# Clustered attention feeding a gated FFN: one pool of eight PSUM banks, five seven-product sets in each later group, and an order read from a table

## The chip, the cores and the metric

The kernel runs on one core of one Trainium2 chip. The metric is device time in microseconds of one execution. TensorE (PE in the profile; its weight loads are PEld), VectorE (DVE), ScalarE (ACT), GpSimd (POOL) and SyncE (SP) each run their own queue of instructions in order and wait for each other through semaphores. TensorE writes its products into PSUM, which has eight banks of 512 float32 per partition; VectorE and ScalarE read them there.

## The reference

There are 4 batches, 8 heads, 768 positions and a head size of 64; 16 centroids per head; d_model 512 and d_ff 1536; 3072 tokens.

```python
q_assign = argmax(einsum(q / |q|, c / |c|));  k_assign = argmax(einsum(k / |k|, c / |c|))
scores = q @ k.T / 8, and -1e9 where q_assign != k_assign
attn   = softmax(scores) @ v                      # [B, H, S, D]
x      = attn.transpose(0, 2, 1, 3).reshape(B * S, H * D)
out    = (sigmoid(x @ w_gate) * (x @ w_val)) @ w_out
```

## The kernel before

**Attention.** The work of a batch `b` is cut into two *groups* of queries (`gr` 0 and 1: even and odd chunks of 128 queries), and each group into four head pairs `p`. One group of one pair is a *block*: 3 chunks of queries, 384 columns (in batch 0 some blocks are split into 2 and 1 chunks, so that there are 36 blocks in all). `prepare`, `prepare_pair` and `prepare_first` turn the queries and keys, find each position's cluster and append it as extra rows of the operands; the products of `scored` in `prepare` (line 687) are the cluster scores for two pairs of heads. `attend` works through the 12 units (head, key chunk) of a block, two units at a time: score products (line 1008) into a tile `sc` of two PSUM banks, one exponential on ScalarE over both banks (line 1032, 768 elements), value products with the exponentials as weights (line 1059, 65 columns each) into the bank `av`. At the end of a block VectorE takes the reciprocal of the row sums out of `av` (line 1084), scales (line 1089), and the result is turned into `x`, by DMA in most blocks.

**FFN.** When the four pairs of a group are done, `feed` multiplies `x` with the gate and value weights. The common form takes one 128-row chunk `fc` of d_ff at a time: four gate products and four value products (line 1396, 384 columns each), Tanh on ScalarE (line 1561) and one VectorE instruction that gates (line 1572). The other form, `seven_products`, takes two chunks `fa`, `fa + 1` at once as a 2 x 2 by 2 x 2 block product with seven products in place of eight: seven times four matmuls of 192 columns (line 1474), three copies of banks on ScalarE (line 1493) and three additions on VectorE (line 1505), then two Tanh (line 1512) and two gating instructions (line 1520). One such *set* replaces sixteen matmuls of 384 columns, two Tanh and two gating instructions. It needs differences of `x` (line 1436, four per group) and sums of the weights, which `sum_up_weights` makes once (line 1377). Before, the groups have 0, 0, 2, 2, 2, 3, 3 and 2 sets, 14 in all; the temporary tiles `pu` and `p5` of a set exist twice each. `project` then multiplies with `w_out`, two 128-token chunks at a time, itself with seven products (line 1271), sums of `hT` on VectorE (line 1241), halvings on ScalarE (line 1289) and sums on VectorE (line 1296), and stores.

**PSUM and order.** The eight banks are two `sc` tiles of two banks, one `av` bank and three `ring` banks for everything else. All steps are tasks of the class `Order`. It runs a list schedule on planned durations: on each engine the task that can start first goes first, and among those within 0.02 us of it the one with the smallest `due`. DMA landing times are computed by `transfers`, and eight rounds of both are made before the instructions are written out:

```python
for _ in range(8):
    order = self.schedule()
    self.transfers()
order = self.schedule()
```

The queue of every engine is therefore fixed when the program is built. A task that acquires a buffer waits for the last user of the buffer's slot; `ring` takes the slot that comes free first, the other tags go round in turn.

Of the kernel before, what the change touches and what calls it, by code (L numbers as in the profile page):

```python
# [9 lines left out]
FP = mybir.dt.float32  # L10
# [3 lines left out]
AX = mybir.AxisListType  # L14

# [23 lines left out]
class Order:  # L39
# [54 lines left out]
    def transfers(self):  # L94


        begin = self.DMA_START
        todo = sorted((t for t in self.tasks if t.dma), key=lambda t: t.start + begin[t.eng])
        queues, left, now, n = {}, {}, 0.0, 0
        while n < len(todo) or any(queues.values()):  # L100
            heads = [ts[0] for ts in queues.values() if ts]
            come = todo[n].start + begin[todo[n].eng] if n < len(todo) else float("inf")
            if heads:
                total = sum(t.pkt for t in heads)
                step = min(min(left[t] * total / t.pkt for t in heads), max(0.0, come - now))
                for t in heads:
                    left[t] -= step * t.pkt / total
                    if left[t] < 1e-6:
                        t.landing = now + step + self.DMA_LAND - t.start
                        queues[t.eng].remove(t)  # L110
                now += step
            else:
                now = max(now, come)
            while n < len(todo) and todo[n].start + begin[todo[n].eng] <= now + 1e-9:
                queues.setdefault(todo[n].eng, []).append(todo[n])
                left[todo[n]] = todo[n].dma
                n += 1
# [92 lines left out]
def kernel(  # L210
# [45 lines left out]
        "xn": ([128, QCH, 128], HP), "x": ([128, NDC, 512], HP), "hT": ([128, NFC, 512], HP),  # L256
        "gt": ([128, 512], FP), "p5": ([128, 384], FP), "out2": ([128, 2, DM], FP),
        "sc": ([128, 2, 512], FP), "av": ([128, 512], FP), "ring": ([128, 512], FP),
    }
    PSUM = bass.MemoryType.PSUM  # L260
    SPACES = {"sc": PSUM, "av": PSUM, "ring": PSUM}
# [4 lines left out]
            (banks if tag in SPACES else const).tile(*SHAPES[tag], name=f"{tag}{i}")  # L266
            for i in range(n)
        ]
        for tag, n in BUFS.items()
# [7 lines left out]
    def take(buf):  # L277
        buf.tile = kept[buf.tag][buf.slot]
        return buf.tile

# [12 lines left out]
    WP = (2, 4, 8)  # L293
    wss = const.tile([128, len(WP), 4, 2, 2, 128], HP, name="wss")
# [56 lines left out]
    w_ring = Buf("av")  # L351
# [66 lines left out]
    c_ring = Buf("av")  # L418
# [160 lines left out]
    def prepare(b, grp, due, step, act=(), queues=("SP",), split=False):  # L579
# [101 lines left out]
        rg = Buf("sc")  # L681

        def scored():
            ps = take(rg)
            for half in range(2):
                for g, (p, nm) in enumerate(sides):
                    nc.tensor.matmul(  # L687
                        out=ps[32 * g : 32 * g + 32, half, :QB], lhsT=cblk[:, 2 * p + half, :],
                        rhs=t32[p, nm].tile[:, half * QB : (half + 1) * QB], start=True, stop=True,
                    )  # L690
# [3 lines left out]
            due, lat=0.3, acq=[rg], uses=[t32[x] for x in sides],  # L694
        )
        for half in range(2):
# [10 lines left out]
            def back(cols=cols, oh=oh, half=half):  # L707
# [5 lines left out]
                lambda t1=t1, half=half: turn_scores(take(t1)[:n], rg.tile[:n, half, :QB]),  # L713
                [cl], due, lat=0.11, acq=[t1], uses=[rg],
# [268 lines left out]
    def attend(block, at, slot):  # L983
# [15 lines left out]
        for i, (e, j) in enumerate(some):  # L999
            kb = aug[b, p][j % 2]  # L1000

            def score(i=i, e=e, j=j, kb=kb):
                ps = sc.tile if i else take(sc)
                to = (
                    ps.rearrange("p u c -> p (u c)")[:, i * N : (i + 1) * N] if together % 2
                    else ps[:, i // per, i % per * N : (i % per + 1) * N]
                )
                nc.tensor.matmul(  # L1008
                    out=to,
                    lhsT=kb.tile[0:80, 0, e * QB + j // 2 * 128 : e * QB + (j // 2 + 1) * 128],  # L1010
                    rhs=qb_.tile[0:80, 1, e * QB + c0 * 128 : e * QB + c0 * 128 + N],
                    start=True, stop=True,
                )
# [6 lines left out]
                    acq=[] if i else [sc], uses=[kb, qb_] + ([sc] if i else []),  # L1020
# [5 lines left out]
        def exponentials():  # L1026
            to, of = take(es)[:, : together * N], sc.tile
            if together % 2:
                of = of.rearrange("p u c -> p (u c)")[:, : together * N]
            else:  # L1030
                to, of = to.rearrange("p (u c) -> p u c", u=2), of[:, :, : per * N]
# [12 lines left out]
            [*t1, c_small, c3], due, lat=0.16, acq=[es], uses=[sc],  # L1044
        )
        first, last = at == 0, at + together == len(UNITS)
        if first:
            avb[block] = Buf("av")
        av = avb[block]
# [3 lines left out]
        def value():  # L1053
# [16 lines left out]
            seq=exps[-1:], acq=[av] if first else [], uses=[es] + ([] if first else [av]),  # L1070
# [52 lines left out]
        t5 = od.add("DVE", 0.12 + 0.113 * nq, norm, [t4], due - 7.0, lat=0.14, acq=[xn], uses=[av, rr])  # L1123
# [62 lines left out]
    def project(b, one, two, final, many, end):  # L1186
# [11 lines left out]
        if many:  # L1198
# [11 lines left out]
            r1, r2 = Buf("sc"), Buf("sc")  # L1210
            X, Y, Z = (lambda: r1.tile[:, 0, :HM]), (lambda: r2.tile[:, 0, :HM]), (lambda: r1.tile[:, 1, :HM])
        else:
            s1, s2, s4, hf, df = (Buf(x) for x in ("s22", "s11", "s12", "half", "diff"))
            t_s1, t_s2, t_s4, t_hf, t_df = (lambda x=x: x.tile for x in (s1, s2, s4, hf, df))
            r1, r2 = Buf("ring"), Buf("ring")
            X, Y, Z = (lambda: r1.tile[:, :HM]), (lambda: r2.tile[:, :HM]), (lambda: r1.tile[:, HM:])

# [82 lines left out]
        def out_part(r, m):  # L1300
# [8 lines left out]
            Z, many, lambda: a(0, 1), lambda i: w_part(i, 1, 0), lambda i: done1[: 2 * i], [], [r1, *hs], runs=parts,  # L1309
# [11 lines left out]
        k2 = halved(lambda: t_df()[:, 1], X, [p6], [], [r1, df], due=due)  # L1321
# [42 lines left out]
    Q2 = {"DVE": nc.vector, "POOL": nc.gpsimd}  # L1364

    def sum_up_weights(n, fa, due):
        g1, g2, v1, v2 = weights(fa)
        s2, s3, s4, s1 = (wss[:, n, i] for i in range(4))
        before = [wload["g"][fa // FPG], wload["v"][fa // FPG]]
        tasks = []  # L1370
        for to, x, y, op in (
            (s1, v1, v2, ALU.add), (s3, g1, v1, ALU.subtract), (s2, s1, g1, ALU.subtract), (s4, g2, s2, ALU.subtract),
        ):
            tasks.append(
                od.add(
                    "DVE", 0.4 if "DVE" == "DVE" else 1.65,
                    lambda to=to, x=x, y=y, op=op: Q2["DVE"].tensor_tensor(to, x, y, op),
                    before + tasks[-1:], due, lat=0.12, both=True,
                )
            )  # L1380
        wsums_of[fa] = [tasks[-1]]

    def feed(b, gr, work):
# [27 lines left out]
        if not wsums_of:  # L1411
# [33 lines left out]
        def seven_products(fa, work):  # L1445
            n = WP.index(fa)
            g1, g2, v1, v2 = weights(fa)
            s2, s3, s4, s1 = (wss[:, n, i] for i in range(4))
            if (b, gr) == (B - 1, 1):
                X = Y = Buf("sc")  # L1450
            else:
                X, Y = Buf("ring"), Buf("ring")
            Z = Buf("ring")
# [3 lines left out]
            def bank(r_, y=0):  # L1457
                return (r_.tile[:, y] if r_.tag == "sc" else r_.tile)[:, :N]
# [7 lines left out]
            def product(r_, new, w_, x_, deps, step, y=0):  # L1466

                def go():
                    if new and not (y and X is Y):
                        take(r_)  # L1470
                    ps = by_chunk(bank(r_, y))
# [9 lines left out]
                    due_ffn(work + step * 0.8), lat=0.25, acq=[r_] if new and not (y and X is Y) else [],  # L1481
                    uses=[xb, tb] + ([r_] if not new or y and X is Y else []), seq=free + ([m1] if y and new else []),
                )

            def copied(i, r_, m, eng="ACT", y=0):
# [3 lines left out]
                def go():  # L1489
                    if new:  # L1490
                        take(to)
                    if eng == "ACT":
                        nc.scalar.copy(held(i), bank(r_, y))  # L1493
                    else:
                        nc.vector.tensor_copy(held(i), bank(r_, y))
# [6 lines left out]
            def added(i, r_, deps, y=0):  # L1502
                return od.add(
                    "DVE", 0.45,
                    lambda: nc.vector.tensor_tensor(held(i), bank(r_, y), held(i), ALU.add), deps,  # L1505
# [27 lines left out]
            m5 = product(Y, True, s1, lambda: t_part(0), [], 0.02, 1)  # L1533
            m2 = product(Z, True, g2, lambda: x_part(1, 0), [], 0.04)
            k1 = copied(0, X, m1)
            k5 = copied(2, Y, m5, "ACT", 1)
            a11 = added(0, Z, [m2, k1])
            m6 = product(X, False, s2, lambda: t_part(1), [k1], 1)
            m3 = product(Y, False, s4, lambda: x_part(1, 1), [k5], 1.02, 1)
            k2 = copied(1, X, m6)  # L1540
            a12 = added(1, Y, [m3, k2], 1)
# [7 lines left out]
        for fc in range(NFC):  # L1549
# [17 lines left out]
            rv, v1 = proj("v", fc, due, [g1])  # L1567

# [97 lines left out]
    z_ring = Buf("av")  # L1666
# [43 lines left out]
```

## Time and profile before

| | |
|---|---|
| time, median of 3 runs | 313.62 us (313.61 to 313.62) |
| the profiled execution's own time | 313.22 us |
| its span, first to last instruction | 311.4 us |
| TensorE clock granted | 1.00 throughout |
| PE busy | 303.7 us, 3251 matmuls |
| PEld busy | 222.8 us |
| ACT busy | 238.2 us, 389 instructions |
| DVE busy | 217.8 us, 532 instructions |
| POOL busy | 77.0 us |

The profiled execution's own time is 1.8 us longer than its span and 0.4 us shorter than the median of the timed runs. A busy time is the time in which at least one instruction of the engine was under way. Successive instructions of an engine overlap by their start-up and their tail, so the distance from one start to the next is shorter than the duration that a row shows; both are used below, the first as *pace*, the second as *duration*.

### The profile page before, as it was taken

The numbers are of one execution on the slowest core, as the hardware profiler recorded it, in microseconds if no ns is written. First come the engines' busy times: TensorE is split into PE (matmuls) and PEld (weight loads), VectorE is DVE, ScalarE is ACT, GpSimd is POOL, SyncE is SP. The second block draws the span as 40 slices with busy tenths as digits, with TensorE's granted clock in tenths as the row PEclk, the third lists the DMA queues.
The fourth block names the chain that finished last, engine by engine and source line by source line (L and its number), as shares of the span: only waits on it lengthen the run. The fifth ranks groups of instructions, "written<-read, shape, count | busy, mean of one in ns | idle before, by whom it ended". The sixth has DMA issues, their size and how long they took to land.

```text
span 311.4 us, 8300 instructions
## 1 busy us (share of the span) xinstructions
PE 303.7 (98%) x3251; PEld 222.8 (72%) x3251; DVE 217.8 (70%) x532; ACT 238.2 (76%) x389; POOL 77.0 (25%) x110
## 2 busy tenths in 40 slices
PE   8998999999999999999999999999999999999995
PEld 3676888544687867757776877757777888778784
DVE  4999945899865739885376938977375824685862
ACT  4799999334999989868997777959899778945531
POOL 4997756751012302440002200570000000000000
PEclk9999999999999999999999999999999999999999
DMA  6999999993356966891465673978300121001003
GB/s 217 359 272 212 214 175 129 163 154 72 69 99 142 114 100 204 106 114 45 107 105 84 101 182 99 103 101 73 96 4 14 48 83 46 15 2 67 2 1 135
DMA packets 97286, 34.49 MB, mean 111 GB/s; under 512 B 83120, under 2 KB 93024, under 8 KB 97248
## 3 DMA queue, kind: packets, MB, share of 16 engines
q1 hardware_dynamic: 72192, 24.57, 34.6%
q0 software_dynamic: 24336, 8.65, 26.4%
q10 hardware_dynamic: 720, 0.75, 0.7%
q8 instruction: 25, 0.41, 0.6%
q14 instruction: 13, 0.11, 0.2%
HBM read 28.34 MB, written 6.29 MB: 111 GB/s over the span
## 4 chain that ended last, share of the span: by engine, by line
PE 92%; ACT 4%; DVE 1%; DMA 1%; issue 0%; SPq 0%; ACTq 0%
PE ring L1396 29%; PE sc L1008 19%; PE ring L1271 16%; PE av L1059 11%; PE ring L1474 9%; ACT es L1032 3%; PE sc L687 3%; PE sc L1271 1%; PE sc L1474 1%; DMA nat<-in_k_dram 1%; PE ring L795 1%; PE ring L617 1%; PE ring L835 1%; PE ring L903 0%; PE ring L948 0%
## 5 line engine op out<-in xcount | busy, mean ns | idle before, releaser
L1032 ACT ACTIVATE es<-sc,nbias 128x768 f16<-128x768 f32 (+1 forms) x189 | 167.8, 925 | 21.2 <-PE sc L1008 20.4
L1059 PEld LDWEIGHTS <-es 128*128 128x128 f16 x1152 | 53.6, 97 | 13.6
L1059 PE MATMUL av<-vp,es 128*128 128x65 f16 x1152 | 58.6, 193 | 0.0
L1396 PE MATMUL ring<-x,wv 128*128 128x384 f16 (+2 forms) x272 | 55.4, 326 | 0.1
L1396 PE MATMUL ring<-x,wg 128*128 128x384 f16 (+2 forms) x272 | 55.3, 326 | 0.0
L1561 ACT ACTIVATE gt<-ring 128x384 f32<-128x384 f32 (+2 forms) x68 | 33.9, 499 | 28.0 <-PE ring L1396 24.8
L1572 DVE SCALAR_TENSOR_TENSOR hT<-gt,ring 128x384 f16<-128x384 f32 (+2 forms) x68 | 37.2, 548 | 24.3 <-PE ring L1396 20.7
L650 POOL CAST even<-t 128x768 f16<-128x768 f32 x24 | 20.6, 875 | 119.9 <-DVE t L595 47.1
L1396 PEld LDWEIGHTS <-wv 128*128 128x128 f16 x272 | 24.7, 97 | 16.5 <-issue 2.1
L1396 PEld LDWEIGHTS <-wg 128*128 128x128 f16 x272 | 24.4, 97 | 14.6 <-issue 0.8
L1271 PEld LDWEIGHTS <-hT 128*128 128x128 f16 x294 | 27.3, 97 | 5.0
L1008 PE MATMUL sc<-even 80*128 80x384 f16 (+2 forms) x120 | 26.1, 293 | 1.6 <-ACT es L1032 0.9
L1008 PE MATMUL sc<-odd 80*128 80x384 f16 x96 | 26.6, 325 | 0.1
L1271 PE MATMUL ring<-wo,hT 128*128 128x256 f16 x198 | 26.4, 272 | 0.0
L1008 PE MATMUL sc<-even,odd 80*128 80x384 f16 (+2 forms) x120 | 26.1, 293 | 0.0
L1008 PE MATMUL sc<-odd,even 80*128 80x384 f16 x96 | 25.8, 326 | 0.0
L1008 PEld LDWEIGHTS <-even 80*128 80x128 f16 x216 | 19.7, 98 | 8.2 <-issue 3.1
L1008 PEld LDWEIGHTS <-odd 80*128 80x128 f16 x216 | 19.7, 98 | 7.3 <-issue 2.1
L595 DVE STREAM_TRANSPOSE t<-nat 128x384 f32<-128x384 f32 x40 | 21.1, 553 | 1.2 <-DMA nat<-in_q_dram 0.9
L1505 DVE TENSOR_TENSOR nat<-ring,nat 128x384 f32<-128x384 f32 x26 | 13.9, 548 | 10.8 <-ACT nat L1493 9.2
L1296 DVE SCALAR_TENSOR_TENSOR out<-ring,diff 128x256 f32<-128x256 f32 x22 | 9.3, 422 | 17.0 <-PE ring L1271 16.8
L1271 PEld LDWEIGHTS <-s 128*128 128x128 f16 x198 | 18.7, 97 | 3.4
(133 smaller groups left out, 444.8 us busy)
## 6 DMA issues: line engine op xcount, KB each, us to landing
out_dram<-out SPq DMA_DIRECT2D x22, 256.0 KB, 2.2
nat<-in_k_dram SPq DMA_DIRECT2D x32, 96.0 KB, 3.0
nat<-in_q_dram SPq DMA_DIRECT2D x32, 96.0 KB, 3.0
odd<-even SPq DMA_DIRECT2D x12, 192.0 KB, 2.9
vp<-in_v_dram POOLq DMA_DIRECT2D x24, 96.0 KB, 4.6
nat<-in_k_dram SPq DMA_DIRECT2D x5, 384.0 KB, 7.7
nat<-in_q_dram SPq DMA_DIRECT2D x5, 384.0 KB, 6.2
nat<-in_v_dram SPq DMA_DIRECT2D x4, 384.0 KB, 7.9
```

The costliest lines, as they stand in the source:

```text
L595: nc.vector.transpose(t[:, half * QB : (half + 1) * QB].rearrange("p (c x) -> p c x", x=128), blocks_[:, half],)
L650: nc.gpsimd.tensor_copy(t[:, NM[nm], cols], t32[p, nm].tile[:, cols])
L687: nc.tensor.matmul(out=ps[32 * g : 32 * g + 32, half, :QB], lhsT=cblk[:, 2 * p + half, :], rhs=t32[p, nm].tile[:, half * QB : (half + 1) * ...
L1008: nc.tensor.matmul(out=to, lhsT=kb.tile[0:80, 0, e * QB + j // 2 * 128 : e * QB + (j // 2 + 1) * 128], rhs=qb_.tile[0:80, 1, e * QB + c0 * ...
L1032: i = nc.scalar.activation(to, of, AF.Exp, bias=nbias, scale=D ** -0.5 if quarters(b, p) else scale,).ins
L1059: nc.tensor.matmul(out=av.tile[:, g : g + D + 1], lhsT=es.tile[:, i * N + c * 128 : i * N + (c + 1) * 128], rhs=vp[:, e, j, :], start=firs ...
L1271: nc.tensor.matmul(out=ps[:, lo:hi], lhsT=left_()[:, i], rhs=right(i)[:, lo:hi], start=new and i == 0, stop=i == NFC // 2 - 1, skip_group_ ...
L1396: nc.tensor.matmul(out=ps[:, :N], lhsT=ws[fc // FPG][:, dcc, fc % FPG, :], rhs=xb.tile[:, dcc, :N], start=(dcc == 0), stop=(dcc == NDC - 1),)
L1474: nc.tensor.matmul(out=ps[:, f], lhsT=w_[:, d, f], rhs=x_()[:, d], start=new and not (f or d), stop=d == 1, skip_group_check=True,)
L1505: lambda: nc.vector.tensor_tensor(held(i), bank(r_, y), held(i), ALU.add), deps,
L1561: lambda rg=rg, gt=gt: nc.scalar.activation(take(gt)[:, :N], rg.tile[:, :N], AF.Tanh, scale=0.5),
L1572: nc.vector.scalar_tensor_tensor(t[:, fc, :N], gt.tile[:, :N], 1.0, rv.tile[:, :N], ALU.add, ALU.mult)
```

## The change

- **One pool.** All eight banks are one tensor `big`, and `ring` has eight slots. A step of two score units, and the cluster scores of `prepare`, acquire any two free slots; the two banks are read as `big[:, lo : hi + 1 : hi - lo]`, so that an exponential or a transposition steps from one bank to the other by whatever distance they have. `sc` (2) and `av` (1) remain as tokens without memory: still at most two score steps and one value bank are open at a time. Exponentials over one bank only are possible too; the first block takes 2, 4, 4 and 2 units at a time in place of 3, 3, 3 and 3.
- **Five sets.** `WP` grows from (2, 4, 8) to (2, 4, 6, 8, 10), and every group of batches 1 to 3 uses all five: 30 sets in place of 14. One of the four weight sums is now written over the value weights `v1`, after the last ordinary use of them in batch 0; the other three have a place of their own, 5 x 3 in place of 3 x 4. `hT` tile 0 is 384 columns wide in place of 512.
- **The order.** `transfers` and its rounds go. Each task gets its rank from a table `PLACES` as `due`, and each DMA its landing time from a table `LANDINGS`; one list schedule with these gives the queues.

The arithmetic of the result, the DMAs and their sizes stay as they are. The core of the diff:

```diff
+PLACES = """ 0 1 9 2 16 3 5 15 ... """        # one rank for each task
+LANDINGS = """ 2.6 3.45 4.13 ... """          # one landing time for each DMA
     def run(self):
-        for _ in range(8):
-            order = self.schedule()
-            self.transfers()
+        places, landings = ([float(x) for x in text.split()] for text in (PLACES, LANDINGS))
+        moved = [t for t in self.tasks if t.dma]
+        for t, at in zip(self.tasks, places):
+            t.due = at
+        for t, landing in zip(moved, landings):
+            t.landing = landing
         order = self.schedule()
...
-        "sc": 2, "av": 1, "ring": 3, "p5": 2,
+        "ring": 8, "p5": 2, "sc": 2, "av": 1,
...
+    big = banks.tile([128, BUFS["ring"], 512], FP, name="ring")
+    kept["ring"] = [big[:, i] for i in range(BUFS["ring"])]
...
+    def both_banks(two):
+        lo, hi = sorted(buf.slot for buf in two)
+        return big[:, lo : hi + 1 : hi - lo]
...
-    WP = (2, 4, 8)
-    wss = const.tile([128, len(WP), 4, 2, 2, 128], HP, name="wss")
+    WP = (2, 4, 6, 8, 10)
+    wss = const.tile([128, len(WP), 3, 2, 2, 128], HP, name="wss")
...
-            together = 3
-        per = together // 2
+            together = 4 if 0 < at < len(UNITS) - 2 else 2
+        per = together // 2 if together * N > 512 else together
...
-        sc, es = Buf("sc"), Buf("es")
+        turn_, sc, es = Buf("sc"), [Buf("ring") for _ in range(together // per)], Buf("es")
...
-            (s1, v1, v2, ALU.add), (s3, g1, v1, ALU.subtract), (s2, s1, g1, ALU.subtract), (s4, g2, s2, ALU.subtract),
+            (s1, v1, v2, ALU.add, []), (s2, s1, g1, ALU.subtract, []), (s4, g2, s2, ALU.subtract, []),
+            (v1, g1, v1, ALU.subtract, raw_users[fa] + raw_users[fa + 1]),
...
-        seven = WP[: {(0, 0): 0, (0, 1): 0, (1, 0): 2, (1, 1): 2, (2, 0): 2, (2, 1): 3, (3, 0): 3, (3, 1): 2}[b, gr]]
-        if (b, gr) == (B - 1, 1):
-            seven = (2, 4)
+        seven = WP if b else ()
...
-            if (b, gr) == (B - 1, 1):
-                X = Y = Buf("sc")
-            else:
-                X, Y = Buf("ring"), Buf("ring")
-            Z = Buf("ring")
+            s3 = v1
+            X, Y, Z = Buf("ring"), Buf("ring"), Buf("ring")
```

More of the change, by code (lines that the diff above doesn't have):

```diff
@@ L92, in free_slots @@
         return max(x[0] for x in ends), [x[1] for x in ends]
[L94 to L111, printed above, removed]
-            else:
[L113 to L117, printed above, removed]
-    def run(self):
-        for _ in range(8):
-            order = self.schedule()
-            self.transfers()
+    def run(self):
+        places, landings = ([float(x) for x in text.split()] for text in (PLACES, LANDINGS))
+        moved = [t for t in self.tasks if t.dma]
+        assert len(places) == len(self.tasks) and len(landings) == len(moved)
+        for t, at in zip(self.tasks, places):
+            t.due = at
+        for t, landing in zip(moved, landings):
+            t.landing = landing
         order = self.schedule()
@@ L1002, in score @@
             def score(i=i, e=e, j=j, kb=kb):
[L1003 to L1007, printed above, removed]
+                to = big[:, sorted(x.slot for x in sc)[i // per], i % per * N : (i % per + 1) * N]
                 nc.tensor.matmul(
@@ L1464, in by_chunk, with product @@
                 return t.rearrange("p (f t) -> p f t", f=2)
-            def product(r_, new, w_, x_, deps, step, y=0):
+            def product(r_, new, w_, x_, deps, step):
                 def go():
-                    if new and not (y and X is Y):
+                    if new:
                         take(r_)
-                    ps = by_chunk(bank(r_, y))
+                    ps = by_chunk(bank(r_))
                     for f in range(2):
@@ L1664 @@
             work = feed(b, gr, work)
-    z_ring = Buf("av")
+    z_ring = Buf("ring")
     def zeros_in_between():
```

100 lines of the change are left out of this document (50 added, 50 removed), and 104 rows, old and new, of tables (LANDINGS, PLACES).

## The prediction

> **What bounds the kernel now.** First the page: busy times, and the chain that ended last.
>
> ```profile
> PE 303.7 (98%) x3251; PEld 222.8 (72%) x3251; DVE 217.8 (70%) x532; ACT 238.2 (76%) x389; POOL 77.0 (25%) x110
> ...
> PE 92%; ACT 4%; DVE 1%; DMA 1%; issue 0%; SPq 0%; ACTq 0%
> ```
>
> TensorE is busy almost throughout and carries 92% of the chain; ScalarE's 4% is early. Since busy time is an average, I next asked for busy time by windows.
>
> ```profile
> 10.00:20.00 10.00, 9.38 (x119) 6.57 (x118) 9.52 (x25) 8.60 (x12) 9.77 (x15) 1.00 1.07 365
> 20.00:30.00 10.00, 9.43 (x130) 7.32 (x129) 9.24 (x26) 9.68 (x13) 8.88 (x13) 1.00 1.20 202
> 30.00:40.00 10.00, 9.49 (x145) 8.33 (x144) 8.73 (x26) 10.00 (x14) 6.88 (x9) 1.00 1.23 211
> 190.00:200.00 10.00, 10.00 (x125) 8.35 (x123) 9.93 (x25) 10.00 (x20) 3.33 (x4) 1.00 0.59 84
> 280.00:290.00 10.00, 9.50 (x92) 8.17 (x91) 6.13 (x14) 5.38 (x14) 0.00 (x0) 1.00 0.14 52
> ```
>
> The columns after the width are PE, PEld, DVE, ACT and POOL. Three stages differ. From 10 to 40 us PE lacks 0.62, 0.57 and 0.51 us, beside a full ScalarE. Later, as from 190 to 200, PE is full; ScalarE and VectorE can be full beside it. Near the end PE waits again, with nobody full. So less PE work pays from about 40 us on, if the others can follow. The next view is the chain in order of time, for PE's pace.
>
> ```profile
> 55.82 1.43 PE sc L687 x16
> ...
> 120.16 0.66 PE ring L1474 x8
> ...
> 159.53 1.30 PE ring L1396 x8
> ```
>
> Back to back, a 192-column matmul takes 0.66 / 8 = 0.0825 us and a 384-column one 1.30 / 8 = 0.1625. The paces of ScalarE and VectorE come from their timelines, start to start:
>
> ```profile
> 119.13 0.49 ACT L1561 ACTIVATE gt<-ring 128x384 f32<-128x384 f32 x1
> 119.50 1.70 ACT L1032 ACTIVATE es<-sc,nbias 128x768 f16<-128x768 f32 x2
> 121.07 0.51 ACT L1493 COPY nat<-ring 128x384 f32<-128x384 f32 x1
> 121.43 0.53 ACT L1493 COPY p<-ring 128x384 f32<-128x384 f32 x1
> 121.80 0.96 ACT L1032 ACTIVATE es<-sc,nbias 128x768 f16<-128x768 f32 x1
> 122.60 0.53 ACT L1493 COPY nat<-ring 128x384 f32<-128x384 f32 x1
> 122.95 0.60 ACT L1512 ACTIVATE nat<-nat 128x384 f32<-128x384 f32 x1
> 123.38 0.96 ACT L1032 ACTIVATE es<-sc,nbias 128x768 f16<-128x768 f32 x1
> ```
>
> ```profile
> 291.96 0.54 DVE L1572 SCALAR_TENSOR_TENSOR hT<-gt,ring 128x384 f16<-128x384 f32 x1
> 292.43 0.55 DVE L1520 SCALAR_TENSOR_TENSOR hT<-nat,p 128x384 f16<-128x384 f32 x1
> 292.89 0.54 DVE L1520 SCALAR_TENSOR_TENSOR hT<-nat,sc 128x384 f16<-128x384 f32 x1
> ```
>
> An exponential of 768 takes (121.07 - 119.50) / 2 = 0.785, a copy 0.365, a Tanh out of PSUM 0.37, one within SBUF 0.43; a VectorE instruction of 384 float32 takes 0.465.
>
> **The sets.** One set takes 28 x 0.0825 = 2.31 us of PE in place of 16 x 0.1625 = 2.60. Sixteen more sets: 16 x 0.29 = **-4.64 us**, all of it in stages where PE is full.
>
> They cost ScalarE 3 copies and 2 Tanh, 3 x 0.365 + 2 x 0.43 = 1.955 us, in place of 2 x 0.37 = 0.74: 16 x 1.215 = +19.4 us. They cost VectorE five instructions in place of two: 16 x 3 x 0.465 = +22.3 us, and eight more weight sums, under 0.47 each, +3.7. Neither is on the path while PE covers it, so I count a later group (four blocks and one feed). For value products I need one more pace; the fence also holds the waits near the end.
>
> ```profile
> 273.24 0.34 PE L1059 MATMUL av<-vp,es 128*128 128x65 f16 x6
> ...
> 274.40 0.53 PE L1059 MATMUL av<-vp,es 128*128 128x65 f16 x12
> ...
> 276.80 0.33 PE L1097 MATMUL ring<-ident,xn 128*128 128x128 f16 x3 [0.25 <-DVE hT L1520]
> ...
> 288.00 0.49 PE L1474 MATMUL sc<-nat,wss 128*128 128x192 f16 x4 [0.50 <-DVE nat L1505]
> ```
>
> Six more value products take 0.19 us, 0.032 each. PE: 48 score products x 0.1625 = 7.8, 144 value products x 0.032 = 4.6, five sets 11.55, two ordinary chunks 16 x 0.1625 = 2.6, the output with 1.5 x 42 matmuls at two thirds of 0.1625, 6.8: together 33.3 us. ScalarE: 24 x 0.785 = 18.8, sets 9.8, two gates 0.7, six halvings under 0.37 each, 2.2: 31.5 us, or 94%. With the present 2.33 sets on average it is 28.3 of 34.1, 83%. PE stays the bound, with a thin cover: 1.8 us a group.
>
> The cover is not even. In the order of instructions of the changed program, counted between the ends of blocks at these paces, ScalarE's work exceeds PE's in four later stretches, by 1.3, 0.6, 1.4 and 1.6 us, 4.9 in all. In the present order there is one such stretch (8.4 against 7.6, before the 31st block ends), and PE shows no wait in it: four `es` buffers let ScalarE run up to 4 x 0.785 = 3.1 us ahead. Bounds 0 and 4.9; nearest is that stretch without a wait, so I take **+0.3**.
>
> **The early stage.** The reciprocals at the ends of the sixth and twelfth block:
>
> ```profile
> 33.56 0.17 DVE L1084 RECIPROCAL rr<-av 128x4 f32<-128x4 f32 x1
> ...
> 54.58 0.19 DVE L1084 RECIPROCAL rr<-av 128x6 f32<-128x6 f32 x1
> ```
>
> These 21.0 us are ScalarE's: 24 exponentials x 0.785 = 18.8 and eight 256-wide gates make 21.0. PE's queue holds 19.8 us there. The changed order puts 22.0 us of PE work beside 21.3 of ScalarE's: the first cluster scores of batch 1 (the 1.43 us at 55.82) move to just behind the sixth block, and two blocks of batch 1 now stand ahead of the long ordinary feed, where PE had 29.1 us beside ScalarE's 11.2 (now 24.5 beside 10.4). PE work done beside exponentials need not be done later: I take **-1.0** of the 1.2 between 21.0 and 19.8. Bounds: 0, if data for the moved steps come late, and -2.2, if another 1.0 of the 1.7 us of waits between 10 and 40 us goes.
>
> The moved cluster scores also move their VectorE chain and, on SP, the shift and the eight row copies, which now queue ahead of batch 1's quarter loads; on POOL the loads for the second half of batch 1 come behind one cast more. Behind those wait the second cluster scores, which stand at the same place of PE's order as now (59 us of PE work in, 60 now), in the ordinary feed, which has other products for PE: 0, at most +1.
>
> **Start, pool, sums.** The first exponential waits for two score products of 256 columns in place of three, -0.1. Exponentials already step over two banks at 0.785; a longer stride I price at 0, both ways. With `sc` and `av` kept as tokens the pool lets no third score step in, so alone it gains nothing in attention; it serves the sets, whose three banks came out of three `ring` slots. The weight sums stand behind the last ordinary use of `v1`, in batch 0's feed: 0.
>
> **The end.** The last feed has no exponentials beside it. From the conversion of `x` that follows the products at 276.80 to the last gating, VectorE's queue holds 15.0 us now and PE's 20.3 to its last product; changed, 20.6 and 21.3. The slack falls from 5.3 to 0.7 us. With 5.3 PE waited 0.25 + 0.50; three sets more, with one such 0.50 each, would be 1.5, and double that is my upper bound. But PE now has output products of the group before between the sets, so I take **+0.6**, bounds 0 and +3.
>
> **Sum.** -4.64 + 0.3 - 1.0 - 0.1 + 0.6 = -4.84 us. The profiled execution took 313.22, 1.8 more than its span and 0.4 under the median of 313.62; the former gives 308.4, the latter, which I forecast, **308.8**.
>
> **Rivals.** The rows on which they rest, groups by shape:
>
> ```profile
> L1032 ACT ACTIVATE es<-sc,nbias 128x768 f16<-128x768 f32 x180 | 158.5, 915 | 20.9 <-PE sc L1008 20.1
> ...
> L1474 PEld LDWEIGHTS <-wss 128*128 128x128 f16 x224 | 19.1, 97 | 2.8 <-issue 0.6
> ...
> L1493 ACT COPY nat<-ring 128x384 f32<-128x384 f32 x24 | 12.2, 508 | 0.4 <-PE ring L1474 0.4
> ```
>
> *The four stretches are not absorbed* (0.13): up to 4.6 us more, 311 to 313.4, say 312.2. For it: order and buffers are fixed. Against it: the present stretch.
>
> *ScalarE becomes the bound; slower* (0.10). The place is the six later groups. An instruction that waits for a bank or for VectorE costs its duration and not its pace: 24 x 0.915 + 5 x (3 x 0.508 + 2 x 0.60) + 2 x 0.49 + 2.2 = 38.8 us a group against 31.5. It passes PE's 33.3 once a quarter of ScalarE's instructions wait so. At a half it is 35.15, and 6 x 1.85 = 11 us on the 308.5 that remain without the +0.3 give 319.6. For it: a set is a chain PE, ScalarE, PE, ScalarE, PE, VectorE, PE, VectorE, and `pu` and `p5` allow two at a time. Against it: from 190 to 200 us, with sets, ScalarE is full and PE too.
>
> *The weight loads set the pace of 192-column matmuls* (0.02). A load takes 0.097 us, more than 0.0825. If they did not overlap, a set would take 28 x 0.097 = 2.72 us, 0.12 more than 2.60: 16 x 0.12 = +1.9, with the other terms 315.3. The row at 120.16 is against it. The Trainium skill speaks for something like it: "TensorE: Matmul & The Clock Gate", Back-to-back issue gap, gives sustained streams of load and matmul about 81 ns each at 128 columns and 131 at 512; by a straight line between them, an estimate of mine, 192 columns would take 89 and 384 take 114, and sixteen sets would cost 10.7 us rather than save any. The trace, with 82.5 and 162.5, disagrees.
>
> *More goes early* (0.07): all 1.7 us of waits before 40 us and nothing lost at the end, 306.0.
>
> *The pool and the table bring nothing*: -4.64 and the two losses, 309.9, which lies in my own case (0.68).
>
> **Numbers.** My own case reaches from 306.7 (-2.2 early, no losses) to 311.2 (the end at +3). With half of the larger gain and most of the unabsorbed stretches the range is 306.2 to 312.6; left out are 0.12 slower, 0.03 and 0.04. A difference of 0.2%, 0.6 us, is about what a measurement can tell from none. Faster: 0.68 + 0.07 + 0.10 of the stretches = 0.85; same 0.03; slower 0.12.
>
> **What would show it.** Right: the new row of set products with 840 matmuls and about 0.33 us per four back to back; ScalarE about 19 us busier and VectorE 25; the sixth block's end near 33 us and the fourteenth's near 66 us, PE full from there to about 270 us; waits of PE on VectorE's additions at the end of 1 to 2 us. Wrong: waits of PE on exponentials or `L1512` after 100 us of more than 1 us in all (ScalarE as the bound), waits on cluster scores before 75 us (late data), or four set products taking more than 0.35 us back to back.

## The result, and the profile after

| kernel | median of its runs, us | lowest to highest | executions |
|---|---|---|---|
| before, beside the changed kernel | 313.62 | 313.37 to 313.62 | 4 |
| changed | 424.71 | 420.15 to 427.52 | 4 |

The changed kernel takes 1.343 times as long, 95% interval 1.3377 to 1.3483, where I had forecast 308.8 us. Two of the four executions, at 427.4 and 427.5 us, ran at a lower granted clock than the others; ratios, sums and the table of experiments leave such executions out, so that this kernel counts with 421.1 us below, and two others with 318.7 (319.7 in the statements) and 631.2. The profiled execution took 422.06 us, its span is 420.3. These are its busy times, the granted clock in 40 slices, and the chain that ended last:

```profile
PE 339.7 (81%) x3443; PEld 250.4 (60%) x3443; DVE 246.2 (59%) x588; ACT 265.7 (63%) x437; POOL 77.8 (18%) x110
...
PEclk9985565999999985899799998999989999999999
...
PE 52%; ACT 27%; DVE 11%; issue 4%; SPq 2%; DMA 2%; POOL 1%; ACTq 0%; DVEq 0%; POOLq 0%
ACT es L1123 23%; PE ring L1099 13%; PE ring L1558 11%; PE ring L1360 9%; PE ring L1485 8%; PE ring L1150 7%; PE ring L782 2%; SPq L429 2%; DVE nat L1589 2%; DVE hT L1604 1%; ACT nat L1596 1%; DVE hT L1657 1%; DMA x<-xn 1%; DVE xn L1180 1%; PE ring L712 1%
```

TensorE fell from 98% to 81% busy, and no other engine rose: ScalarE went from 76% to 63%. The busy times of ScalarE and VectorE grew by 27.5 and 28.4 us (I had 19.4 and 26.0). Part of that is instructions that stand apart and no longer overlap: in the kernel without the waits, below, the growth is 17.9 and 24.1. No engine has become the bound; they stand still in turn. ScalarE has 27% of the chain in place of 4%, nearly all of it in the exponentials. The waits, longest sums first (us in total, times, longest):

```profile
PE ring L1099 <- ACT es L1123: 29.6, 40, 1.4
...
ACT es L1123 <- PE ring L1099: 24.9, 34, 2.2
...
DVE hT L1657 <- ACT es L1123: 18.9, 8, 9.0
...
PE ring L1558 <- ACT es L1123: 15.0, 20, 1.1
...
ACT es L1123 <- PE ring L1485: 12.2, 12, 2.2
```

The third, fourth and fifth rows make no sense as data flow. A set's products (L1558) don't use the exponentials, an exponential doesn't use ordinary FFN products (L1485), and a gating instruction on VectorE (L1657) uses neither. All that the two sides share is that they touch PSUM. A bank that is handed on can make such a wait too, but of all the waits that the built program draws between these pairs of lines only 1 of 11 (third row), 5 of 26 (fourth) and 0 of 17 (fifth) join instructions with a bank in common. The exponentials themselves, in the groups by shape, are no slower than the 915 ns before:

```profile
L1123 ACT ACTIVATE es<-ring,nbias 128x768 f16<-128x768 f32 x176 | 155.4, 902 | 75.7 <-PE ring L1099 15.5 <-PE ring L1150 13.8 <-PE ring L1485 12.2
```

The windows of 10 us (after the width: PE, PEld, DVE, ACT, POOL, then the granted clock) show a second thing:

```profile
10.00:20.00 10.00, 8.97 (x105) 5.96 (x105) 9.13 (x23) 8.16 (x12) 9.22 (x13) 1.00 1.09 347
30.00:40.00 10.00, 7.11 (x62) 5.13 (x61) 3.94 (x11) 4.44 (x4) 0.30 (x1) 0.50 1.22 197
160.00:170.00 10.00, 7.35 (x42) 4.32 (x41) 2.42 (x5) 4.50 (x7) 0.83 (x1) 0.50 0.18 49
```

Where PE has long gaps its granted clock falls to 0.50, and then the products that do run take longer. In the last of these windows four 384-column products last from 166.69 to the next start at 167.97, 0.32 us each, against the 0.1625 of the kernel before:

```profile
166.69 1.48 PE L1485 MATMUL ring<-x,wg 128*128 128x384 f16 x4
167.97 0.52 PE L1099 MATMUL ring<-odd 80*128 80x384 f16 x1
```

### The profile page after: what moved, and what is told of

Same layout as the page of the kernel before. It is cut to its first block, busy times and chain, and to the rows that moved or that the text cites. A ratio compares the mean times of both kernels' runs of the same rounds, so it can differ in the third digit from the quotient of the medians.

```text
span 420.3 us, 8801 instructions
## 1 busy us (share of the span) xinstructions
PE 339.7 (81%) x3443; PEld 250.4 (60%) x3443; DVE 246.2 (59%) x588; ACT 265.7 (63%) x437; POOL 77.8 (18%) x110
## 4 chain that ended last, share of the span: by engine, by line
PE 52%; ACT 27%; DVE 11%; issue 4%; SPq 2%; DMA 2%; POOL 1%; ACTq 0%; DVEq 0%; POOLq 0%
ACT es L1123 23%; PE ring L1099 13%; PE ring L1558 11%; PE ring L1360 9%; PE ring L1485 8%; PE ring L1150 7%; PE ring L782 2%; SPq L429 2%; DVE nat L1589 2%; DVE hT L1604 1%; ACT nat L1596 1%; DVE hT L1657 1%; DMA x<-xn 1%; DVE xn L1180 1%; PE ring L712 1%
## 5 line engine op out<-in xcount | busy, mean ns | idle before, releaser
L1123 ACT ACTIVATE es<-ring,nbias 128x768 f16<-128x768 f32 (+2 forms) x189 | 168.8, 912 | 91.3 <-PE ring L1099 24.9
L1150 PE MATMUL ring<-vp,es 128*128 128x65 f16 x1152 | 63.0, 202 | 12.2 <-ACT es L1123 12.0
L1657 DVE SCALAR_TENSOR_TENSOR hT<-gt,ring 128x256 f16<-128x256 f32 (+2 forms) x36 | 19.5, 551 | 37.9 <-ACT es L1123 18.9
L1558 PEld LDWEIGHTS <-wss 128*128 128x128 f16 x360 | 31.0, 98 | 11.8 <-issue 9.8
L1099 PE MATMUL ring<-even 80*128 80x384 f16 (+2 forms) x120 | 29.8, 321 | 9.6 <-ACT es L1123 6.7
L1099 PE MATMUL ring<-even,odd 80*128 80x384 f16 (+2 forms) x120 | 30.4, 326 | 7.5 <-ACT es L1123 7.5
L1485 PE MATMUL ring<-x,wg 128*128 128x256 f16 (+2 forms) x144 | 32.3, 355 | 4.6 <-ACT es L1123 4.1
L1558 PE MATMUL ring<-x,wg 128*128 128x192 f16 x240 | 30.1, 251 | 6.6 <-ACT es L1123 5.3
L1558 PE MATMUL ring<-nat,wv 128*128 128x192 f16 x240 | 29.8, 247 | 6.7 <-ACT es L1123 5.6
L1596 ACT ACTIVATE nat<-nat 128x384 f32<-128x384 f32 x60 | 31.0, 526 | 4.4 <-DVE nat L1589 4.2
L1485 PE MATMUL ring<-x,wv 128*128 128x256 f16 (+2 forms) x144 | 31.4, 348 | 0.6 <-ACT es L1123 0.6
L1558 PE MATMUL ring<-nat,wss 128*128 128x192 f16 x240 | 29.3, 248 | 2.9 <-ACT es L1123 2.9
```

The costliest lines, as they stand in the source:

```text
L1099: nc.tensor.matmul(out=to, lhsT=kb.tile[0:80, 0, e * QB + j // 2 * 128 : e * QB + (j // 2 + 1) * 128], rhs=qb_.tile[0:80, 1, e * QB + c0 * ...
L1123: i = nc.scalar.activation(to, of, AF.Exp, bias=nbias, scale=D ** -0.5 if quarters(b, p) else scale,).ins
L1150: nc.tensor.matmul(out=av.tile[:, g : g + D + 1], lhsT=es.tile[:, i * N + c * 128 : i * N + (c + 1) * 128], rhs=vp[:, e, j, :], start=firs ...
L1485: nc.tensor.matmul(out=ps[:, :N], lhsT=ws[fc // FPG][:, dcc, fc % FPG, :], rhs=xb.tile[:, dcc, :N], start=(dcc == 0), stop=(dcc == NDC - 1),)
L1558: nc.tensor.matmul(out=ps[:, f], lhsT=w_[:, d, f], rhs=x_()[:, d], start=new and not (f or d), stop=d == 1, skip_group_check=True,)
L1596: lambda: nc.scalar.activation(held(i), held(i), AF.Tanh, scale=0.5), [m], due_ffn(work), lat=0.16,
```

## Theories

**A, waits for banks in between.** The change makes the eight banks one tensor, and an exponential reads `big[:, lo : hi + 1 : hi - lo]`. If the ordering that is drawn between instructions takes such a read as all banks from `lo` to `hi`, each exponential is ordered against whoever uses the banks in between, though it never touches them. Counted in the semaphore waits of the built programs, the changed kernel has 302 waits between PE, ScalarE and VectorE in which the two sides share no bank, but one lies in the range of the other; in each of them one side is an exponential. The Trainium skill, "PSUM — Partial Sum Buffer", PSUM bank collisions raise a hardware error, gives the reason why PSUM is ordered by bank at all: two engines in one bank and quadrant at a time are an error, so one guards "by bank × quadrant (by bank is the simple version), not by address". By that rule a bank that is stepped over needs no guard; no run here shows a collision.

**Rivals.** *S*: ScalarE's read over far banks is slow by itself. *T*: the order of the table or the five sets make the loss, and the pool doesn't. *E*: five sets make ScalarE the bound (my own slower rival). *C*: the low clock is the cause and not the consequence.

## The experiments

All times are medians, each beside runs of the kernel before on the same chip (313.3 to 313.6 us). The column of waits counts those of theory A.

| kernel | waits | us | ratio, 95% interval |
|---|---|---|---|
| before, one tensor, neighbouring pairs (b_near) | 0 | 313.5 | 0.9969 to 1.0016 |
| the same, one bank in between (b_mild) | 230 | 358.0 | 1.1414 to 1.1448 |
| the same, five banks in between (b_far) | 608 | 631.2 | none given |
| changed, list schedule in place of the table (l_any) | 305 | 406.8 | 1.2937 to 1.3 |
| changed, neighbours, list schedule (l_five) | 0 | 318.1 | 1.0137 to 1.0203 |
| changed, an exponential for each bank (a_split) | 0 | 325.2 | 1.0337 to 1.0395 |
| changed, neighbouring pairs (a_adjacent) | 0 | 318.7 | 1.01 to 1.0215 |
| changed, own order, neighbours but for 9 pairs (a_exact) | 25 | 321.6 | 1.0255 to 1.0292 |
| the same, those 9 split (a_intent) | 0 | 316.3 | 1.006 to 1.0118 |
| the same, three SP issues moved (a_intent_x) | 0 | 314.0 | 1.0018 to 1.0048 |
| a_adjacent with the three SP issues moved (a_xfirst) | 0 | 312.0 | 0.995 to 0.9982 |
| a_xfirst with three score steps at a time (a_sc3) | 0 | 313.3 | 0.9965 to 1.0011 |
| changed, fixed division of banks (a_fixed) | 0 | 321.5 | 1.0226 to 1.0271 |
| the same, list schedule (l_fixed) | 0 | 320.7 | 1.0196 to 1.0246 |

### Only bank numbers, in the kernel before

Instructions and order of all engines are the same in the three kernels; only bank numbers differ. (Against the kernel before, the first block's exponentials are cut differently too.)

```diff
+    big = banks.tile([128, 8, 512], FP, name="ring")
+    kept["sc"] = [big[:, lo : hi + 1 : hi - lo] for lo, hi in ((0, 1), (2, 3))]   # far: ((0, 6), (1, 7)); mild: ((0, 2), (3, 5))
+    kept["av"] = [big[:, 4]]                                                      # far: 2; mild: 6
+    kept["ring"] = [big[:, i] for i in (5, 6, 7)]                                 # far: 3, 4, 5; mild: 1, 4, 7
```

> The kernel before, its order and its instructions, with the eight banks allocated as one tensor; each pair for the exponentials is two neighbouring banks (0 and 1, 2 and 3), the accumulator is bank 4, the three single buffers banks 5 to 7. The first block's twelve units go through six exponentials of two units in place of four of three, so that none runs over a bank's end. All theories: 313 to 316 us, as before. It is the control for the next one.

> The same as the control, but for the bank numbers: the pairs are banks 0 and 6, and 1 and 7, the accumulator is 2, the single buffers are 3 to 5. Theory A (an exponential over two banks by a stride is ordered against everything that touches the banks in between, although it doesn't touch them): 608 such waits are drawn between the engines here, and none in the control, so over 370 us, with PE and ScalarE waiting on each other by name and the row of the 128x768 exponential near its 915 ns. Theory S (the read itself is slow over far banks): the row of the 128x768 exponential grows well over 915 ns and the time by 180 times that growth at most. Theory T (five sets of products and the table of places made the loss, the pool didn't): 313 to 316 us.

> The kernel before in its own order, as in the far version, but the pairs are banks 0 and 2, and 3 and 5: one bank in between, a single buffer each time (1 and 4; 7 is the third, 6 the accumulator). 230 waits for a bank in between in place of 608. Theory A: between the two, some 340 to 440 us (440 if the loss goes by the number of waits: 339 x 230 / 608 = 128). Theories S and T: 313 to 316 us.

One tensor with neighbours costs nothing. With five banks in between the time more than doubles. Of the far kernel the busy times, its clock, three waits and the group of its exponentials:

```profile
PE 447.9 (71%) x3251; PEld 284.3 (45%) x3251; DVE 222.6 (35%) x532; ACT 254.7 (40%) x391; POOL 76.9 (12%) x110
...
PEclk9555555569855555556965597699986799796999
```

```profile
ACT es L1033 <- PE ring L1272: 86.1, 48, 3.2
...
ACT es L1033 <- PE ring L1397: 80.4, 51, 4.6
...
PE ring L1009 <- ACT es L1033: 76.4, 89, 1.3
```

```profile
L1033 ACT ACTIVATE es<-ring,nbias 128x768 f16<-128x768 f32 x176 | 158.6, 901 | 264.5 <-PE ring L1272 86.1 <-PE ring L1397 80.4 <-PE ring L1060 29.5
```

In the near kernel PE waits for exponentials for 1.0 us in all, and the same group reads:

```profile
PE ring L1009 <- ACT es L1033: 1.0, 3, 0.4
```

```profile
L1033 ACT ACTIVATE es<-ring,nbias 128x768 f16<-128x768 f32 x176 | 155.5, 914 | 17.8 <-PE ring L1009 16.7
```

901 against 914 ns: the read over far banks is not slow, so S falls, and T can't explain this pair at all, since it has neither five sets nor the table. The mild kernel's two timelines show one such wait (start, duration, engine, line):

```profile
120.92 1.72 ACT L1033 ACTIVATE es<-ring,nbias 128x768 f16<-128x768 f32 x2
```

```profile
121.90 0.81 PE L1272 MATMUL ring<-nat,s 128*128 128x256 f16 x6 [0.38 <-ACT es L1033]
```

The first of the two exponentials ends about 0.9 us after 120.92, and an output product, which has nothing to do with it, starts just then. Its granted clock stays full:

```profile
PEclk9999999999999999999999999999999999999999
```

So 44.5 us are lost without any loss of clock, and C falls as a first cause. Per wait that is 0.19 us; in the far kernel (631.2 - 313.5) / 608 = 0.52, with the clock at 0.72. The low clock is a part of that difference; how large a part, the last section estimates.

### Table or no table

```diff
-        places, landings = ([float(x) for x in text.split()] for text in (PLACES, LANDINGS))
-        ...
+        for _ in range(8):
+            order = self.schedule()
+            self.transfers()
         order = self.schedule()
```

> The changed kernel (any two banks by a stride, five sets) without the tables: order by the list schedule with the due times of the kernel before. 305 waits for banks in between are drawn, against 302 with the table. Theory A: the table has no part in the loss, 400 to 440 us. Theory T (the table's order makes the loss): 318 us, as the version with neighbouring banks and the list schedule.

The second kernel has the list schedule too, and `free_slots` gives out only neighbours where two banks are asked for:

```diff
+            if count == 2:
+                pairs = [(max(a[0], b[0]), a, b) for a, b in zip(ends, ends[1:]) if None not in (a[0], b[0])]
+                ends = list(min(pairs)[1:]) if pairs else []
```

> The version with neighbouring banks and five sets, but without the tables: the order comes from the list schedule with the due times and the modelled transfers of the kernel before. If the table's order is worth something: 320 to 335 us, slower than the 319.7 with it. If the table costs: 308 to 314 us.

With nearly the same number of waits (305) the list schedule loses nearly as much, and with neighbours 88.7 us of it are gone. So the table doesn't make the loss. My statement on the second kernel, that 320 to 335 us would show the table to be worth something, wasn't met, and neither was the other one: at 318.1 us the list schedule can't be told from the table with neighbours below (318.7; the intervals of the two overlap).

### The same banks, one at a time

```diff
+            parts = [(to, of)]
+            if len(sc) == 2:
+                parts = [(to[:, u], big[:, s, : per * N]) for u, s in enumerate(sorted(x.slot for x in sc))]
+            made = [nc.scalar.activation(t, o, AF.Exp, ...).ins for t, o in parts]
```

> The changed kernel, its order and its choice of banks, with each exponential over two banks made as two instructions, one for each bank; so none covers a bank that it doesn't read. From the rows of 128x768 (902 ns) and 128x1024 (1113 ns) a half of 384 columns takes about 586 ns by estimate, so ScalarE is busy some 50 us longer, 316 us. Theory A: 330 to 360 us, ScalarE now the bound. Theory S: the same. Theory T: 425 us or more. Theory C (the low granted clock is the first cause): 420 us or more, with the clock still at 0.5 in the first stages.

PE, VectorE, GpSimd and SP have the changed kernel's order, and the banks are the same; ScalarE has 187 instructions more. The loss falls from 107 to 12 us, a bit more than I expected; ScalarE's busy time is 278.1 us and not my 316, since halves follow each other faster than their durations. It now sets the pace where exponentials run, as in this window, where it is full (fourth number) and PE isn't:

```profile
120.00:130.00 10.00, 9.32 (x104) 6.96 (x102) 6.51 (x15) 10.00 (x25) 3.53 (x5) 1.00 0.43 119
```

### Neighbours, with the table

> The changed kernel with one edit: where two of the eight banks are asked for, they must be neighbours (the pair of neighbours that comes free first); five sets and table as they are. No bank lies between the two. Theory A: most of the loss goes, 305 to 320 us (my forecast of 308.8 stands for what is left), and the waits of PE on exponentials fall from 29.6 us at the score products to under 5. Theory S: the same. Theory T: 415 to 430 us. Theory E (ScalarE has become the bound by five sets): 340 us or more, with ScalarE busy over 80%.

102.4 us of 107.5 go with the choice of neighbours (the edit in `free_slots` above, the table kept; the order shifts a little, since slots come free at other times, and the next kernel keeps it). PE's waits on exponentials at the score products fall from 29.6 us to 1.4. T and E fall as causes of the loss: five sets and the table are all there. But 318.7 is 9.9 over my forecast. One wait stands out; SP's queue and PE's timeline show it:

```profile
205.09 0.53 SPq L753 DMA_DIRECT2D odd<-even  x1
205.73 0.52 SPq L433 DMA_DIRECT2D out_dram<-out  x1
206.34 0.50 SPq L753 DMA_DIRECT2D odd<-even  x1
206.94 1.71 SPq L1212 DMA_TRANSPOSE x<-xn  x1
```

```profile
214.11 0.32 PE L1489 MATMUL ring<-x,wg 128*128 128x384 f16 x1 [3.62 <-DMA x<-xn]
```

The last transposition into `x` is issued behind two shifts and a store, and PE can start 7.2 us after its issue. The table's landing time for it is 2.85.

> The changed kernel with the same instructions in the same order on every engine; only the bank numbers are given out anew along that order, neighbours where two are asked for (9 pairs, for which no neighbours were free, stay apart). 25 waits for banks in between are left of 302. Theory A (these waits are the loss): 308 to 325 us. Theory T (the order of the table doesn't suit the chip, in which case the neighbour version before won by its changed order): over 380 us.

```diff
         order = self.schedule()
+        self.neighbours(order)      # the order stays; banks are given out anew along it
```

The changed kernel with its own order, where all but 9 pairs are neighbours, takes 321.6: T falls again. The waits left were more than I took them for, as the next one shows.

### What is left without such waits

> The version with the changed kernel's own order on every engine and banks given out anew, and the 9 exponentials whose banks still lie apart are made as two instructions each, one for each bank: no wait for a bank in between is left (25 before). This is the change without such waits. If the 25 waits carry most of what the version before it had over my forecast (321.6 against 308.8): 309 to 315 us. If the order of the table costs it (the wait for the transposition of x, SP's queue): 317 to 321 us.

The 9 pairs that lie apart get two instructions each, as in the split kernel above. The last 25 waits were worth 5.4 us, 0.21 each. The time lies between the two ranges of my statement. This kernel is the change without waits for banks in between, and it is 0.9% slower than before. So 421.1 - 316.3 = 104.8 us of the loss are these waits and what follows from them. Its busy times:

```profile
PE 302.6 (96%) x3443; PEld 235.9 (75%) x3443; DVE 241.9 (77%) x588; ACT 256.1 (81%) x446; POOL 77.9 (25%) x110
```

The spans of the two profiles differ by 420.3 - 315.0 = 105.3 us, for the same products in the same order: 37.1 of it is more busy time of PE (339.7 - 302.6) and 68.2 time without a product. Of the 37.1, some 28 are the low clock by an estimate (PE's busy time times the share of the clock that was not granted, summed over windows of 2.5 us). The rest fits products that stand apart and no longer overlap: the mild kernel's PE is 14.0 us busier than the near one's (318.1 against 304.1) at full clock.

```diff
+        for u in (1357, 1360, 1281):                      # two shifts and a store
+            self.behind(self.tasks[u], [self.tasks[1716]])  # behind the transposition
```

> The same, with the three issues on SP behind the transposition of x, as in the version that took 312.0 us. If both matter: 307 to 312 us, 3 to 6 us under the run beside it; if the transposition isn't late here: the same time as that run.

> The version with neighbouring banks, and behind one transposition of x by DMA (the one at 206.9 us, for which PE waited 3.6 us at 210.5) go the three issues on SP that stood ahead of it, two shifts and one output. Theory X (the table's order of SP's queue costs what the neighbour version is slower than forecast; after the wait the clock is low too): the wait goes and the time falls by 4 to 6 us, to 313 to 316. Rival (the remaining loss is spread over ScalarE's stretches): 318 to 320 us.

The first gains 2.3 us, less than the 3 to 6 I expected, the second 6.7, a little more than the 4 to 6. 312.0 us is the one version that is faster than before, by 0.34% (interval 0.18 to 0.50).

### Is the pool worth its banks

> Five sets alone, as nearly as can be: list schedule, and the banks divided again, banks 0 and 1 and banks 2 and 3 for pairs, 4 to 7 for everything that needs one (accumulator included). If the five sets save what I forecast (4.64 us of PE) and the division is no hindrance: 309 to 312 us. If the sets crowd ScalarE and VectorE: 316 to 320, as the list schedule with neighbours from the pool (318.1).

> Table and five sets, with the banks divided as in the version before this one (two fixed pairs, four single banks), in place of neighbours out of the pool. If the pool itself brings something: slower than the 319.7 of the neighbour version, 321 to 330. If it brings nothing: 312 to 320.

> The version with neighbours and the moved SP issues (312.0 us), with three score steps allowed to hold banks in place of two. If ScalarE's waits for score products (6.6 us in that version) still cost: 309 to 311.5 us. If the third pair takes banks that the sets need: 313 to 318.

```diff
+                pairs = [... for a, b in (ends[0:2], ends[2:4]) ...]     # pairs: banks 0-1 or 2-3
+                ends = sorted(x for x in ends[4:] if x[0] is not None)   # single buffers: 4 to 7
```

Five sets on divided banks are 7 to 8 us slower than the 14 sets before, with either order. Out of a pool of neighbours they are 2.6 (list; the intervals just touch) and 2.9 (table) faster than divided. So the pool brings the sets some 3 us, and even with it they gain little. A third score step brought nothing: the wait of exponentials for score products was 8.0 us against 6.6.

## Why the prediction was wrong

**The step that failed** is one sentence of "Start, pool, sums": "Exponentials already step over two banks at 0.785; a longer stride I price at 0, both ways." The duration indeed didn't grow (902 ns, and 901 over five banks, against 915). I priced the instruction and not what it is ordered against, and that cost some 105 us (421.1 against 316.3). The two banks of `sc` were neighbours and tensors of their own, and no other buffer lay in their range; the change put up to six banks there. What I named as a sign of being wrong, waits of PE on exponentials after 100 us of more than 1 us, is what the profile shows, but I had tied it to ScalarE as the bound. It wasn't: 63% busy.

The other steps can be read from the kernel without such waits, profile against profile (span 315.0 against 311.4). Its windows of 30 us:

```profile
10.00:40.00 30.00, 28.58 (x358) 20.09 (x357) 28.60 (x75) 27.00 (x35) 24.59 (x34) 1.00 1.10 245
...
100.00:130.00 30.00, 29.52 (x358) 23.01 (x356) 21.89 (x51) 28.20 (x47) 9.98 (x13) 1.00 0.78 147
130.00:160.00 30.00, 30.00 (x364) 24.74 (x362) 23.33 (x55) 27.30 (x51) 0.72 (x1) 1.00 0.60 78
160.00:190.00 30.00, 29.48 (x363) 23.08 (x362) 26.19 (x60) 27.27 (x48) 3.91 (x4) 1.00 0.51 96
190.00:220.00 30.00, 27.86 (x330) 22.50 (x328) 25.06 (x60) 24.03 (x46) 9.80 (x12) 1.00 0.95 108
220.00:250.00 30.00, 29.47 (x369) 25.67 (x367) 21.68 (x48) 29.41 (x57) 0.00 (x0) 1.00 0.13 34
250.00:280.00 30.00, 28.47 (x360) 23.91 (x357) 17.57 (x40) 28.02 (x52) 0.00 (x0) 1.00 0.12 32
280.00:315.00 35.00, 30.93 (x318) 27.88 (x315) 27.34 (x68) 17.56 (x42) 0.00 (x0) 0.98 0.17 62
```

Before, from 100 to 280 us PE is full in all of these windows but the last, and the end reads:

```profile
10.00:40.00 30.00, 28.31 (x390) 22.22 (x390) 27.49 (x75) 28.28 (x37) 25.52 (x36) 1.00 1.17 260
...
250.00:280.00 30.00, 29.69 (x327) 23.09 (x325) 16.39 (x37) 23.80 (x42) 0.00 (x0) 1.00 0.13 38
280.00:315.00 35.00, 27.14 (x238) 21.72 (x236) 18.84 (x48) 12.18 (x29) 0.00 (x0) 0.99 0.13 46
```

- **The sets, -4.64.** Their price was right: four products start 0.33 us apart, as at 122.12, 122.45 and 122.78 in this kernel's timeline:

```profile
122.12 0.49 PE L1594 MATMUL ring<-nat,wss 128*128 128x192 f16 x4
122.45 0.49 PE L1594 MATMUL ring<-x,wg 128*128 128x192 f16 x4
122.78 0.49 PE L1594 MATMUL ring<-nat,wss 128*128 128x192 f16 x4
```

  But PE's busy time fell by 1.0 us only (303.67 to 302.64), and by 3.6 in the version of 312.0 us (300.1). Counted from all starts in the two traces, each shape at its median pace, the products themselves come to 284.3 us before and 280.1 after, 4.2 less; the delays between them that are too short to show as idle, since the product before is still in its tail, grew from 19.1 to 22.4 us (19.6 in the version of 312.0). So the saving came, and such delays took most of it back; what holds each product is not settled.
- **ScalarE's stretches, +0.3 of bounds 0 to 4.9.** From 100 to 280 us PE lacks 0.48 + 0 + 0.52 + 2.14 + 0.53 + 1.53 = 5.20 us, against 0.31 before: +4.9. The 2.14 from 190 to 220 are put down to DMA, 1.5 to the late transposition and 0.6 to a store; moving SP's issues took 2.3 us off the time, and I had not priced SP's queue there. Of the rest, 2.4 are waits for exponentials (0.5, 0.4, 0.7 and 0.8 us), beside a ScalarE that is 27 to 29 of 30 us busy. So this term was mis-sized, and for about half of it the rival of the four stretches that are not absorbed was nearer. That ScalarE's load alone sets these waits is not shown: from 220 to 280 us the kernel with neighbouring pairs has ScalarE as busy (57.9 of 60 us) and lacks 0.30 us of PE, where this one lacks 2.06.
- **The early stage, -1.0.** PE lacks 1.42 us from 10 to 40, against 1.69: -0.3, between 0 and the value I took. I had read all three windows there as "beside a full ScalarE"; from 10 to 20 us it was busy for 8.60 of 10, less than VectorE (9.52) and GpSimd (9.77).
- **The end, +0.6.** From 280 us on PE lacks 4.07 of 35.0 against 4.26 of 31.4: -0.2. PE's one wait there before, 0.50 us for an addition on VectorE, is gone, and no other came in its place. That it was the output products between the sets which covered VectorE's chains is not shown.
- **The start, -0.1.** Before 10 us PE lacks 1.67 us against 1.47: +0.2.

Together -1.0 + 4.9 - 0.3 - 0.2 + 0.2 = +3.6, the difference of the spans, where my terms gave -4.84. So even without the false waits the change as written would have been slower, and the forecast of 308.8 too low by 7.5 us beside 316.3. *The weight loads* set no pace (0.33 above). *The pool and the table bring nothing* was wrong in both directions: as written the pool cost some 105 us, and with neighbours the sets were some 3 us faster than on divided banks.

Taking away the waits alone, with the far banks kept and read by one instruction, was not tried.

## What to carry to other kernels

An access by a stride has two prices: its duration, and everything that it is ordered against; before such a read is priced at nothing, count in the built program's waits who stands between, and on what shared bank. Buffers that are read together belong side by side, or in tensors of their own. An instruction that is found waiting for another with which it shares no data is the mark to look for in the list of waits; whether the two share a buffer that was handed on is then seen in the built program.

## What the runs showed of the hardware

The exponential over two banks takes 901 to 914 ns whether the banks are neighbours or six apart. The granted clock fell to 0.50 in windows in which PE had long gaps, and there a 384-column product took 0.32 us in place of 0.1625. What a wait for a bank in between cost rose as the mean clock fell: 0.19 us each at 1.00 (358.0 us), 0.29 at 0.983 (406.8: 88.7 / 305), 0.35 at 0.915 (421.1: 104.8 / 302) and 0.52 at 0.72 (631.2: 317.7 / 608). The clock is only part of it. Some 6, 28 and 127 us of the last three losses are busy time that the low clock added, by the estimate with windows of 2.5 us above; without them a wait cost 0.27, 0.25 and 0.31 us. The Trainium skill, "TensorE: Matmul & The Clock Gate", Part 1: The HAM clock gate, gives the clock two states only, half and full, by how busy PE was over windows of about 3.4 us. The two rows of 0.50 above agree, and a slice with a digit between 5 and 9 in the rows of the clock would then be a mixture of both.
